# Two accumulation chains change places at the end of a 49-product in-projection

## The chip, the cores and the metric

The kernel runs on one core of a Trainium2 chip. The time is the device time of one launch in microseconds (us), as the median of several executions. A profile is one execution taken by the hardware profiler; its times run from the start of its span.

The engines are called TensorE (PE in the profile; its weight loads are PEld), VectorE (DVE), ScalarE (ACT), GpSimd (POOL) and SyncE (SP, which here only issues DMAs). TensorE writes PSUM, which is used as eight banks of 128 x 512 float32. The other engines work between PSUM and SBUF; in this kernel GpSimd only touches SBUF.

## The reference

Routed attention (4 batches, 8 heads, 768 positions, head size 64) is followed by a two-layer block on its 3072 x 512 output. The change touches only the second part, which computes

```
h  = x @ w_in                          # 3072 x 512 by 512 x 2048
sp = max(h, 0) + log1p(exp(-abs(h)))   # softplus
g  = h * erf(sp)
out = g @ w_out                        # 3072 x 2048 by 2048 x 512
```

## The kernel before

The attention takes about the first 430 us. Then the block runs in six chunks of 512 tokens (n = 0 to 5). Each chunk has an in-projection, which makes h transposed, a gate (Softplus, Erf, and a multiplication by h), and an out-projection.

**Fewer products by sums.** The projections are multiplied in the Strassen-Winograd manner: of 2 x 2 blocks, seven products instead of eight, at the price of sums and differences of blocks before and after. Chunks 3, 4 and 5 (`n >= TWICE`) use two such levels in the in-projection, 7 x 7 = 49 products; this is `hidden49` (line 1074). Chunks 1 and 2 run `hidden26`, with one level. Chunks 1 to 5 take the out-projection as 26 products (`project26`, line 1188).

**Slots.** `SLOTS` (line 118) lists the 49 products (i, o) in the order in which they run. i is the outer product and selects the weight form (`w_twice`); o is the inner one and selects the form of x. The list has three groups: i = 1 and 2 (slots 0 to 13), i = 6, 7 and 4 (slots 14 to 34), i = 5 and 3 (slots 35 to 48). In the last group the two chains run interleaved: (5,1), (3,1), (5,5), (3,5), (5,6), (3,6), (5,3), (3,3), (5,7), (3,7), (5,2), (3,2), (5,4), (3,4). A slot is four matmuls of 128 x 128 by 128 x 128 float32, recorded as eight.

**Banks and blocks.** The products of one i share banks: o = 1, 6, 7, 4 accumulate one after another into one bank, o = 5, 3 into a second, o = 2 has its own. The result must be read from the bank between two of them, so the next product of the chain waits for that reader. The results build up h in four pairs, called x, u, w and a fourth, y here (`WHERE`, line 115, gives the first three). Each has four blocks g11, g12, g21, g22 of 128 x 512.

**What follows a slot.** `copied` (line 1090): after o = 1, 5 and 6 ScalarE copies the bank to a place t (for x, w and u in this order); for i = 3 GpSimd then adds t to g12. `feed` (line 1104): after o = 2, 7 and 3, for i = 3 VectorE adds the bank to g12; for i = 5 VectorE adds the bank to t, and GpSimd then adds t to g22 and to g12. `feed_last` (line 1126): after o = 4 VectorE adds the bank to blocks of y: g12 for i = 3, g22 and g12 for i = 5. All of this is one line in the profile, L130, a helper that keeps each engine's instructions in program order. So an instruction that waits holds all that come later on its engine.

**Work between slots.** The table `also` (line 1145) places other work after given slots. `soft1`, `erf1`, `products1` gate the first half of the early blocks (half of h, called lot 0, is finished early), `soft2`, `erf2`, `products2` the second half; one Softplus or Erf works on 128 x 1024, and one product on 128 x 512 (four for each half). Their curves stand in one buffer, `a_s`; its pool has one place, so the next user of it (`soft_late`, line 1045, after slot 47) can't write before the fourth of `products2` has read it. `soft_late(n, 1)` is the Softplus of two late quarters of h; `gate_after` (line 1054) continues with two more, and then Erf and products during `project26`. `first_steps` are three sums of gated blocks (first entries of `LEFT_STEPS`, line 73); the third of them makes the left operand of the out-product p = 2 (`LEFT`, line 69: 17, 13, 18, ...). It writes the place that the copies (3,x) and (3,u) held before. The out-product p = 1 needs the second of `products2`, p = 8 and p = 9 need late products and further steps.

Softplus and Erf have different tables on ScalarE; the compiler puts a table load in front of an instruction whose function is not in the table that is loaded.

**Weight forms.** The second level needs differences of weight blocks. `forms_twice` (line 962) makes those for i = 5, 6 and 4 on GpSimd during chunk 2, in four places (the two `osb` buffers, halved), and stores them to `w_dram` on SP's queue; `hidden49` reads them back in a ring (`load_twice`). The form for i = 7 stays in SBUF: `last_form_twice` (line 976) writes it over b12, seven subtractions on GpSimd between the in- and the out-projection of chunk 2.

In the step numbers below "slot" counts from 0 to 48 in a chunk, and p from 0 to 25 in its out-projection.

Of the kernel before, what the change touches and what calls it, by code (L numbers as in the profile page):

```python
# [9 lines left out]
F32 = mybir.dt.float32  # L10
# [5 lines left out]
ACT = mybir.ActivationFunctionType  # L16
# [3 lines left out]
P = 128  # L20
# [16 lines left out]
FG = HF // 2  # L37
# [76 lines left out]
STEPS = (1, 5, 6, 3, 7, 2, 4)  # L114
WHERE = {"x": (0, 0), "u": (0, 1), "w": (1, 1)}
TWICE = 3
GROUPS = (((1, 2), (1, 5, 6, 3, 7, 2, 4)), ((6, 7, 4), (1, 2, 5, 6, 3, 7, 4)), ((5, 3), (1, 5, 6, 3, 7, 2, 4)))
SLOTS = [(i, o) for inner, outer in GROUPS for o in outer for i in inner]
STREAMED = [s for s in SLOTS if s[0] in (4, 5, 6)]

# [18 lines left out]
def kernel(  # L139
# [10 lines left out]
    nc = tc.nc  # L150

    in_order = [True]
    te, ve, ae, ge = (
        InOrder(tc, e, in_order) for e in (nc.tensor, nc.vector, nc.scalar, nc.gpsimd)
    )
# [6 lines left out]
    dram = pool("dram", 1, space=bass.MemoryType.DRAM)  # L162
# [102 lines left out]
    for base, pattern, sign, op, fill in (  # L265
# [5 lines left out]
            out=first, in_=first, compare_op=op, fill=fill, base=base, pattern=pattern,  # L271
# [19 lines left out]
    places = [x_of[n][:, i : i + 2].rearrange("p k t -> p (k t)") for n in range(2) for i in (0, 2)]  # L291
# [327 lines left out]
    def minus_of(out, a, b, engine=ve):  # L619
        engine.tensor_tensor(out=out, in0=a, in1=b, op=ALU.subtract)  # L620
# [74 lines left out]
    def onto(out, m, engine=ve):  # L695
        plus_of(out, m, out, engine)
# [118 lines left out]

    ring, extra = [], []
    x_extra, spare_more = {}, []
    w_dram = dram.tile([len(STREAMED), P, FG * P], F32, name="w_dram")
    b_dram = dram.tile([N_STREAM + len(KEPT), P, FG * HM], F32, name="b_dram")

    def w_block(b):
# [140 lines left out]
    def forms_twice():  # L962
        places = [outp.tile([P, 2, DM], F32, name="osb").rearrange("p h m -> p (h m)") for _ in range(2)]
        places = [t[:, i * FG * P : (i + 1) * FG * P] for t in places for i in range(2)]
        n = 0
        for o in STEPS:
            w = lefts(*w_in_parts(0, HF))[o]
            b11, b12, b21, b22 = (w[:, k, f * FG * P : (f + 1) * FG * P] for k in range(2) for f in range(2))
            new = [places[(n + i) % 4] for i in range(3)]
            n += 3  # L970
            for i, form, a, b in ((5, minus_of, b12, b11), (6, minus_of, b22, new[0]), (4, minus_of, new[1], b21)):
                t = new[{5: 0, 6: 1, 4: 2}[i]]
                form(t, a, b, ge)
                nc.sync.dma_start(out=w_dram[STREAMED.index((i, o))], in_=t)

    def last_form_twice():
        for o in STEPS:
            w = lefts(*w_in_parts(0, HF))[o]
            b12, b22 = (w[:, k, FG * P :] for k in range(2))
            minus_of(b12, b22, b12, ge)  # L980

    def x_twice(n):
        own = x_of[n].rearrange("p (k i) (t j c) -> p k i t j c", k=2, i=2, j=2, c=P)
# [90 lines left out]
    def hidden49(n):  # L1074
        if banks[0] is None:
            banks[:] = [psb.tile([P, 512], F32, name="bank") for _ in range(6)] + turned
        k = n_banks[0] + 1
        free = [banks[(k + i) % len(banks)] for i in range(len(banks))]
        x_extra[n] = xp.tile([P, DM // P, CT], F32, name="x_own")
        x_forms, x_form = x_twice(n)  # L1080
        for lot in range(2):
            for s in range(2):
                g_of[n, s, lot] = gp.tile([P, 2, 2, FG, P], F32, name="g")
        kept = [outp.tile([P, 2, DM], F32, name="osb").rearrange("p h m -> p (h m)") for _ in range(2)]
        kept = [t[:, i * FG * P : (i + 1) * FG * P] for t in kept for i in range(2)]
        temps = [columns(extra[i]) for i in range(3)] + kept
        fixed = {(5, "x"): kept[0], (5, "w"): kept[1], (5, "u"): kept[2], (3, "x"): temps[2], (3, "w"): kept[3], (3, "u"): temps[2]}
        chain, second, held = {}, {}, {}

        def copied(i, which, m):  # L1090
            t = held[i, which] = fixed[i, which] if (i, which) in fixed else temps.pop(0)
            ae.copy(out=t, in_=m)
            if i == 3:
                ge_onto(gs(WHERE[which])[1], t)

        def gs(c):

            h, s = c
            return [columns(block_of(n, h, s, lot, tt)) for tt in range(2) for lot in range(2)]

        def ge_onto(out, a):
            ge.tensor_tensor(out=out, in0=out, in1=a, op=ALU.add)

        def feed(i, which, m):
            g11, g12, g21, g22 = gs(WHERE[which])
            if i == 3:
                onto(g12, m)
                return
            t = held.pop((i, which))
            dst = {1: g12, 2: g11, 7: g22, 4: g21}.get(i, t)  # L1110
            plus_of(dst, m, t)
            if i == 2:
                ge_onto(g11, g12)
            elif i == 6:
                ge_onto(g12, t)
            elif i == 7:
                ge_onto(g22, g12)
            elif i == 4:
                minus_of(g21, g22, g21, ge)
            elif i == 5:  # L1120
                ge_onto(g22, t)
                ge_onto(g12, t)
            if (i, which) not in fixed:
                temps.append(t)

        def feed_last(i, m):
            g11, g12, g21, g22 = gs((1, 0))
            if i == 1:
                ae.copy(out=g12, in_=m)
            elif i == 2:  # L1130
                plus_of(g11, m, g12)
            elif i in (6, 3):
                onto(g12, m)
            elif i == 7:
                plus_of(g22, m, g12)
            elif i == 4:
                minus_of(g21, g22, m)
            else:
                onto(g22, m)
                onto(g12, m)  # L1140

        soft1, erf1, products1 = gate_early(n, 0)
        soft2, erf2, products2 = gate_early(n, 1)
        first_steps = [functools.partial(left_step, n, x) for x, step in enumerate(LEFT_STEPS) if step[0] < 0]
        also = {
            0: x_forms[0:2], 1: x_forms[2:3], 2: x_forms[3:4], 3: x_forms[4:6], 4: x_forms[6:7], 5: x_forms[7:8],
            10: [soft1[1]], 14: [soft1[0]], 15: [erf1[1]], 16: [erf1[0]],
            20: products1[0:1], 21: products1[1:2], 22: products1[2:3], 23: products1[3:4],
            33: [soft2[1]], 36: [soft2[0]], 37: first_steps[0:1], 38: first_steps[1:2], 40: [erf2[1], erf2[0]],
            43: products2[0:1], 44: products2[1:2], 45: products2[2:3] + first_steps[2:], 46: products2[3:4],  # L1150
            47: [functools.partial(soft_late, n, 1)],
        }
        for at, (i, o) in enumerate(SLOTS):
            w, x = w_twice(n, i, o), x_form(i, o)
            if o in (1, 2, 5):
                m = free.pop(0)
                if o != 2:
                    (chain if o == 1 else second)[i] = m
            else:
                m = (second if o == 3 else chain)[i]  # L1160
            for j in range(FG):
                te.matmul(
                    m[:, j * P : (j + 1) * P], lhsT=w[:, j * P : (j + 1) * P], rhs=x,
                    start=(o in (1, 2, 5) and j == 0), stop=(j == FG - 1), skip_group_check=True,
                )
            if (i, o) in STREAMED:
                k = STREAMED.index((i, o))
                if k + 6 < len(STREAMED):
                    load_twice(n, k + 6)
                else:  # L1170
                    for j in range(RING):
                        tile_of = (N_STREAM * (n - 1) + j + 2) % RING
                        if max(q for q in range(len(STREAMED)) if tile_twice(n, q) == tile_of) == k:
                            load_stream(N_STREAM * (n - 1) + j)
            if o in (1, 5, 6):
                copied(i, {1: "x", 5: "w", 6: "u"}[o], m)
            elif o == 4:
                feed_last(i, m)
            else:
                feed(i, {2: "x", 7: "w", 3: "u"}[o], m)  # L1180
            if o in (2, 3, 4):
                free.append(m)
            for f in also.get(at, ()):
                f()
        banks[:] = free
        n_banks[0] = len(banks) - 1
# [235 lines left out]
    for e in range(2):  # L1422
        ve.tensor_copy(
            out=ccT[e * D : (e + 1) * D, :, e * C : (e + 1) * C],
            in_=pct[e * D : (e + 1) * D].rearrange("d (r e c) -> d r e c", e=2, c=C)[:, :, e],
# [171 lines left out]
```

## Time and profile before

| | before |
|---|---|
| median of 3 executions | 993.03 us (992.92 to 994.28) |
| the profiled execution | 994.45 us |
| its span | 992.7 us |
| PE busy | 964.9 us (97%) |
| DVE, ACT, POOL busy | 780.3 us, 545.8 us, 532.3 us |
| ACT table loads | 42 by the compiler, 1283 ns each |
| chunk 4, slots 0 to 46 and before (793.4 to 836.0) | PE busy 42.29 of 42.60 us |
| chunk 4, slot 47 to p = 8 (836.0 to 861.5) | PE busy 20.75 of 25.50 us, clock 0.87 |
| chunk 4, p = 9 and on (861.5 to 891.3) | PE busy 29.79 of 29.80 us |

The timeline's rows give start, duration, engine, line, operation, and the program's names of output and inputs (`bank` and `turned` are PSUM banks; `g` is h; `g_more`, `osb` and `x_own` are places that are used in turn for several things). In brackets stands the idle time of the engine before the row and what ended it.

The chain of waits is followed back from the last instruction. Its rows give start, duration, and the engine or cause. The table of stretches gives, for each, its length, each engine's busy share, the granted clock of TensorE (1.00 is full), the share of the DMA engines and GB/s.

### The profile page before, as it was taken

Reading aid. Unit: us, or ns where it says so; the run is one execution under the profiler, and the core shown is the slowest. Engines: PE = TensorE matmul, PEld = TensorE weight load, DVE = VectorE, ACT = ScalarE, POOL = GpSimd, SP = SyncE. Lnnn points to the kernel's source line nnn. Section 1 sums busy time; section 2 is a strip of 40 time slices with the busy share of each in tenths; the row PEclk is TensorE's granted clock in tenths of the full one; section 3 lists DMA queues with packets and bytes.
Section 4 is the critical chain, followed back from the end, with each engine's and each line's share of the span. In section 5 each row is a group of like instructions: output and inputs, shape, how many; then the busy total and the mean of one; then the engine's idle time right before and its main releaser. Section 6 shows DMA issues by size and latency. Waiting matters only on the chain.

```text
span 992.7 us, 22118 instructions
## 1 busy us (share of the span) xinstructions
PE 964.9 (97%) x8786; PEld 731.5 (74%) x8786; DVE 780.3 (79%) x1372; ACT 545.8 (55%) x835; POOL 532.3 (54%) x368
## 2 busy tenths in 40 slices
PE   8999999999999999999999999989989998999898
PEld 3555555555555555788888888878987898789877
DVE  8888888888888886889698785778757965796577
ACT  3777777777776665585424523542635263526351
POOL 1688888787888888662499306530361037003700
PEclk9999999999999999999999999999999999999999
DMA  9444444444444210331024535214451445243423
GB/s 220 82 110 108 109 108 113 110 116 104 95 95 108 53 34 18 109 112 52 1 86 178 183 136 193 107 52 140 138 192 64 146 131 181 67 164 120 128 85 106
DMA packets 169287, 110.53 MB, mean 111 GB/s; under 512 B 131040, under 2 KB 140768, under 8 KB 169184
## 3 DMA queue, kind: packets, MB, share of 16 engines
q1 hardware_dynamic: 166688, 108.69, 38.1%
q8 instruction: 69, 1.13, 0.5%
q10 hardware_dynamic: 2496, 0.43, 0.2%
q14 instruction: 34, 0.28, 0.1%
HBM read 84.71 MB, written 24.38 MB: 110 GB/s over the span
## 4 chain that ended last, share of the span: by engine, by line
PE 89%; ACT 4%; DVE 3%; POOL 2%; issue 1%; DMA 1%; POOLq 0%; DVEq 0%; ACTq 0%; SPq 0%
PE bank L130 38%; PE turned L130 29%; PE sc L130 16%; PE wide L130 6%; POOL g L130 2%; ACT a_s L130 1%; ACT x_own L130 1%; DVE nmx L130 1%; ACT L130 1%; DVE osb L130 1%; DVE g L130 1%; ACT g_more L130 0%; ACT osb L130 0%; DMA g_more<-b_dram 0%; DVE g_more L130 0%
## 5 line engine op out<-in xcount | busy, mean ns | idle before, releaser
L130 POOL TENSOR_TENSOR more_out<-more_out,pr 128x768 f32<-128x768 f32 x128 | 217.1, 1696 | 18.5 <-ACT pr L130 10.0
L130 DVE TENSOR_REDUCE nmx<-wide 128x2 f32<-128x768 f32 x189 | 180.6, 955 | 47.8 <-PE wide L130 47.0
L130 ACT ACTIVATE pr<-sc 128x768 f32<-128x768 f32 x192 | 148.9, 811 | 93.9 <-PE wide L130 77.0
L130 PE MATMUL turned<-pr,in_v 128*32 128x193 f32 x3072 | 144.8, 330 | 0.0
L130 PEld LDWEIGHTS turned<-pr,in_v 128*32 128x32 f32 x3072 | 91.5, 109 | 50.7 <-issue 21.3
L130 POOL TENSOR_TENSOR g<-g 128x512 f32<-128x512 f32 x27 | 35.4, 1311 | 162.4 <-DVE g L130 161.0
L130 PE MATMUL sc<-qT,kT 64*128 64x384 f32 x528 | 98.3, 486 | 0.0
L130 DVE TENSOR_TENSOR g<-a_s,g 128x512 f32<-128x512 f32 x84 | 75.9, 926 | 21.6 <-ACT a_s L130 21.6
L130 ACT ACT_TABLE_LOAD x42 | 53.9, 1283 | 65.8 <-DVE g L130 65.2
L130 DVE TENSOR_TENSOR g<-g 128x512 f32<-128x512 f32 x114 | 78.9, 692 | 13.5 <-PE bank L130 12.1
L130 DVE TENSOR_TENSOR g<-bank,g 128x256 f32<-128x256 f32 (+1 forms) x133 | 58.6, 457 | 38.1 <-POOL g L130 13.0
L130 PE MATMUL bank<-g_more,g 128*128 128x256 f32 x336 | 79.8, 380 | 3.5 <-ACT g_more L130 3.5
L130 PE MATMUL bank<-x_own,w_in 128*128 128x256 f32 (+1 forms) x416 | 77.5, 327 | 0.0
L130 POOL TENSOR_TENSOR more_out<-pr,pr 128x768 f32<-128x768 f32 x32 | 60.3, 1886 | 28.3 <-ACT pr L130 28.3
L130 PEld LDWEIGHTS bank<-g_more,g 128*128 128x128 f32 x336 | 63.3, 190 | 13.9 <-ACT g_more L130 4.7
L130 PE MATMUL bank<-w_out,g 128*128 128x256 f32 x296 | 69.3, 380 | 0.0
L130 PEld LDWEIGHTS bank<-x_own,w_in 128*128 128x128 f32 x416 | 64.2, 191 | 6.0 <-issue 0.6
L130 PEld LDWEIGHTS <-qv 64*128 64x128 bf16 x384 | 27.0, 93 | 52.9 <-issue 36.8
L130 PEld LDWEIGHTS sc<-qT,kT 64*128 64x128 f32 x528 | 49.9, 187 | 21.4 <-ACT inv L130 2.4
L130 PE MATMUL wide<-kv,qv 64*128 64x384 bf16 x378 | 64.0, 328 | 1.4 <-DVE nmx L130 0.6
L130 ACT ACTIVATE a_s<-g 128x1024 f32<-128x1024 f32 (+1 forms) x38 | 42.7, 1146 | 37.6 <-POOL g L130 34.6
L130 PE MATMUL wide<-km,qm 64*128 64x384 bf16 (+1 forms) x378 | 62.6, 327 | 0.0
(235 smaller groups left out, 2051.5 us busy)
## 6 DMA issues: line engine op xcount, KB each, us to landing
g_more<-b_dram SPq DMA_DIRECT2D x48, 512.0 KB, 3.2
g_more<-w_dram SPq DMA_DIRECT2D x63, 256.0 KB, 2.8
x_own<-in_moe_w_in_dram SPq DMA_DIRECT2D x13, 512.0 KB, 4.5
in_v<-in_v_dram SPq DMA_DIRECT2D x32, 192.0 KB, 3.0
x_dram<-more_out SPq DMA_DIRECT2D x128, 48.0 KB, 1.9
x_own<-x_dram SPq DMA_DIRECT2D x6, 1024.0 KB, 5.5
in_k<-in_k_dram SPq DMA_DIRECT2D x59, 96.0 KB, 2.6
in_q<-in_q_dram SPq DMA_DIRECT2D x58, 96.0 KB, 2.6
```

Of the source, the lines that this page charges most:

```text
L130: ins = getattr(self.engine, name)(*args, **kw)
```

## The change

Five things are done:

1. The last group of slots runs i = 3 before i = 5: (3,1), (5,1), (3,5), (5,5) and so on to (3,4), (5,4).
2. The bank copies of (3,w) and (5,w), after slots 37 and 38, go from ScalarE to VectorE. The add of t to g12 after (5,2) goes from GpSimd to VectorE.
3. The Softplus table is loaded by an instruction of its own after slot 8 and after slot 40.
4. In `also`, the first two `first_steps` come after slots 35 and 36 (before: 37 and 38), the first Erf after slot 38 (before: 40), `products2` after slots 42, 44, 46 and 48 (before: 43 to 46), and the third first step after slot 48, behind the fourth product (before: slot 45).
5. `forms_twice` also makes and stores the form for i = 7 (28 subtractions and stores instead of 21), and `last_form_twice` loads it over b12 with seven DMAs of 256 KB instead of subtracting in place.

```diff
-GROUPS = (((1, 2), (1, 5, 6, 3, 7, 2, 4)), ((6, 7, 4), (1, 2, 5, 6, 3, 7, 4)), ((5, 3), (1, 5, 6, 3, 7, 2, 4)))
+GROUPS = (((1, 2), (1, 5, 6, 3, 7, 2, 4)), ((6, 7, 4), (1, 2, 5, 6, 3, 7, 4)), ((3, 5), (1, 5, 6, 3, 7, 2, 4)))
...
-    w_dram = dram.tile([len(STREAMED), P, FG * P], F32, name="w_dram")
+    w_dram = dram.tile([len(STREAMED) + len(STEPS), P, FG * P], F32, name="w_dram")
...
-            new = [places[(n + i) % 4] for i in range(3)]
-            n += 3
-            for i, form, a, b in ((5, minus_of, b12, b11), (6, minus_of, b22, new[0]), (4, minus_of, new[1], b21)):
-                t = new[{5: 0, 6: 1, 4: 2}[i]]
-                form(t, a, b, ge)
-                nc.sync.dma_start(out=w_dram[STREAMED.index((i, o))], in_=t)
+            new = [places[(n + i) % 4] for i in range(4)]
+            for t, i, a, b in (
+                (new[0], 5, b12, b11), (new[1], 6, b22, new[0]), (new[2], 4, new[1], b21), (new[3], 7, b22, b12),
+            ):
+                minus_of(t, a, b, ge)
+                k = STREAMED.index((i, o)) if i < 7 else len(STREAMED) + STEPS.index(o)
+                nc.sync.dma_start(out=w_dram[k], in_=t)
 
     def last_form_twice():
         for o in STEPS:
             w = lefts(*w_in_parts(0, HF))[o]
-            b12, b22 = (w[:, k, FG * P :] for k in range(2))
-            minus_of(b12, b22, b12, ge)
+            nc.sync.dma_start(out=w[:, 0, FG * P :], in_=w_dram[len(STREAMED) + STEPS.index(o)])
...
             t = held[i, which] = fixed[i, which] if (i, which) in fixed else temps.pop(0)
-            ae.copy(out=t, in_=m)
+            if which == "w" and i in (3, 5):
+                ve.tensor_copy(out=t, in_=m)
+            else:
+                ae.copy(out=t, in_=m)
...
                 ge_onto(g22, t)
-                ge_onto(g12, t)
+                if which == "x":
+                    onto(g12, t)
+                else:
+                    ge_onto(g12, t)
...
-            10: [soft1[1]], 14: [soft1[0]], 15: [erf1[1]], 16: [erf1[0]],
+            8: [functools.partial(ae.preload_act_table, ACT.Softplus)], 10: [soft1[1]], 14: [soft1[0]], 15: [erf1[1]], 16: [erf1[0]],
             20: products1[0:1], 21: products1[1:2], 22: products1[2:3], 23: products1[3:4],
-            33: [soft2[1]], 36: [soft2[0]], 37: first_steps[0:1], 38: first_steps[1:2], 40: [erf2[1], erf2[0]],
-            43: products2[0:1], 44: products2[1:2], 45: products2[2:3] + first_steps[2:], 46: products2[3:4],
-            47: [functools.partial(soft_late, n, 1)],
+            33: [soft2[1]], 35: first_steps[0:1], 36: [soft2[0]] + first_steps[1:2], 38: [erf2[1]],
+            40: [erf2[0], functools.partial(ae.preload_act_table, ACT.Softplus)],
+            42: products2[0:1], 44: products2[1:2], 46: products2[2:3], 47: [functools.partial(soft_late, n, 1)],
+            48: products2[3:4] + first_steps[2:],
```

## The prediction

> **What bounds the kernel now.** I read the page's chain of waits first. TensorE sets almost the whole span, so only the places where TensorE is idle or slow can give time back:
>
> ```profile
> PE 89%; ACT 4%; DVE 3%; POOL 2%; issue 1%; DMA 1%; POOLq 0%; DVEq 0%; ACTq 0%; SPq 0%
> ```
>
> The changed slots run in chunks 3, 4 and 5. One chunk lasts 97.8 us: the out-product p=9 starts at 763.75, 861.51 and 959.28 us in the timeline of PE. I work in chunk 4. TensorE runs slots 35 to 46 without a gap and ends slot 46 at 835.7. Up to p=9 it has two slots of 0.89 and nine products of 1.73 us to do, 17.3 us; it needs 25.8. So 8.5 us per chunk are lost there, and that is all this change can win back. The chain of waits, in order of time, names who holds them:
>
> ```profile
> 836.18 0.69 DVE osb L130
> 836.94 2.87 POOL g L130 x2
> 839.87 0.57 issue
> 840.44 0.68 DVE g L130
> 841.12 0.61 DVE osb L130
> 841.80 3.33 POOL g L130 x2
> 845.15 1.30 DVE g L130 x2
> 846.54 1.28 ACT L130
> 847.84 0.66 ACT a_s L130
> ```
>
> VectorE hands a block to GpSimd, waits for it, hands over the next, then ScalarE loads a table and starts Softplus. The timeline of VectorE shows the queue behind it:
>
> ```profile
> 835.57 0.69 DVE L130 TENSOR_TENSOR g<-bank,g 128x512 f32<-128x512 f32 x1 [3.55 <-POOL g L130]
> ...
> 839.83 0.69 DVE L130 TENSOR_TENSOR g<-turned,g 128x512 f32<-128x512 f32 x1 [2.37 <-POOL g L130]
> ...
> 842.23 1.76 DVE L130 TENSOR_TENSOR g_more<-g,g_more 128x512 f32<-128x512 f32 x1
> 845.15 0.69 DVE L130 TENSOR_TENSOR g<-bank,g 128x512 f32<-128x512 f32 x1 [1.16 <-POOL g L130]
> 845.76 0.68 DVE L130 TENSOR_TENSOR g<-a_s,g 128x512 f32<-128x512 f32 x1
> ```
>
> The first, second and fourth rows are slots 42, 44 and 46, chain i=3: they add into the same g12 block into which GpSimd has just been told to add i=5 (slots 41, 43, 45). The last row is the fourth early product; it reads the only a_s buffer, and the late Softplus writes that buffer next:
>
> ```profile
> 846.54 1.28 ACT L130 ACT_TABLE_LOAD   x1 [11.75 <-DVE g L130]
> 847.84 2.01 ACT L130 ACTIVATE a_s<-g 128x1024 f32<-128x1024 f32 x2
> ```
>
> The load starts 0.10 us after that product ends (845.76+0.68=846.44). Chunks 3 and 5 repeat it (748.67 to 748.77, 944.21 to 944.31), so the end T of the fourth product, not the slots' copies, releases ScalarE. From Softplus's start to p=9 it is 861.51-847.84=13.67 us of four Softplus, a load, four Erf and VectorE's work behind them. So p=9 = T+0.10+1.30+13.67.
>
> **Part 1, i=3 before i=5.** No count changes. Now the i=3 add into g12 stands ahead of the i=5 adds to the same block, so VectorE's three waits above (3.55, 2.37, 1.16) go. What is late next: slot 41, now (3,3), adds into the u block's g12, and GpSimd must first add the u copy of slot 39 there. So I follow ScalarE from 826.56, where Softplus still starts on the same GpSimd add: copies of slots 35 and 36 at 827.5 and 828.0, Softplus 828.46 to 829.53, the Erf load moved forward 829.54 to 830.82, Erf to 831.89, u copy of slot 39 from 831.79 to 832.38. GpSimd adds it, 1.27 (row 830.58): 833.7. VectorE starts slot 41 at 833.73. Before, the same kind of wait ended at 835.54.
>
> From there VectorE has fourteen instructions up to the fourth product: nine with a bank as operand (slots 41 to 47 one each, slot 48 two), the added g12 add of (5,x), and four products. Their pitch is 0.60 (841.03, 841.63, 842.23), so 8.45 us and T=842.2 if nothing holds them.
>
> **The price of GpSimd beside them.** Two rows speak. An add from SBUF alone took 1.76 while GpSimd's two took 3.32 (rows 842.23 and 841.80) instead of 0.68 and 2.50: they take turns. Adds with a bank operand keep 0.69 in the same company (820.46). Five GpSimd adds now fall into this stretch (both of u, both of w, one of x), and five VectorE instructions are from SBUF alone. No row shows this order. Below: no collision, T=842.2. Above: each of the five waits out a whole add, 5x1.27=6.35, T=848.55. I take turns, one after the other, as those rows do: product 1 at 834.93 goes first; product 2 at 836.73 meets GpSimd's end, no loss; the (5,x) add waits to 838.6; product 3 waits 839.13 to 840.4; product 4, at 842.65, waits for GpSimd's last add until 843.45. T=844.05, nearer to the lower end.
>
> **Part 2, tables.** The load at slot 40 lands 833.8 to 835.1 on an idle ScalarE, so Softplus follows T directly: 1.30 less. The other load, moved to slot 8, saves nothing: in the trace it already ran at 799.62, 5 us ahead of its Softplus, while GpSimd was awaited. Without the cover of that idle ScalarE each costs 1.28. [...]
>
> **Part 3, the copies of (3,w) and (5,w) on VectorE.** Two bank copies, bounded by a half-size bank copy, 0.42, and a full add, 0.69; I take 0.69, the size. They fall at 827.8 and 828.6, where VectorE was idle 3.46 us (row 831.33). Cost nothing; the cover gone, 1.2. They take 0.9 us off ScalarE ahead of the u copies, which is in the times above.
>
> **Part 4, first step 3 moved behind product 4.** The third out-product, p=2, needs it: 844.05+0.65=844.7. TensorE ends p=1 near 841.5, so it idles 3.2 us there. From 844.7 seven products of 1.725 reach p=9 at 856.8, before ScalarE's path (844.05+0.05+13.67=857.8). But a gap can slow TensorE. The trace has such a case after gaps of 1.22 and 2.50 us (slot 48, p=0 and p=1 in PE's timeline, then one microsecond of the table of stretches, where the number after the five engines is the granted clock):
>
> ```profile
> 840.58 2.08 PE L130 MATMUL turned<-g_more,w_in 128*128 128x128 f32 x8 [2.50 <-DVE g L130]
> 842.45 3.62 PE L130 MATMUL bank<-more_out,g_more 128*128 128x256 f32 x8
> 845.86 1.98 PE L130 MATMUL bank<-w_out,g 128*128 128x256 f32 x8
> ```
> ```profile
> 844.00:845.00 1.00, 1.00 (x3) 0.74 (x3) 0.00 (x0) 0.00 (x0) 1.00 (x1) 0.50 0.00 0
> ```
>
> The clock (the 0.50) is halved for some 5 us, and 3.62 instead of 1.89 is one product's price. Chunk 2's gap of 2.10 us (663.32) brought no loss. Paid again, p=9 moves to 856.8+1.73=858.5, 0.8 later; I take 0 and keep 0.8. [...]
>
> **Part 5, resident forms.** Seven more GpSimd subtractions with seven 256 KB stores in chunk 2; seven reloads replace the seven in-place subtractions. The 21 old ones run 604.1 to 633.1, so 28 end near 644, still before the osb places are wanted (first write after 650). While they run, VectorE's four products at 634.89 to 638.02 lengthen from 0.69 to 1.42, as at 620.22 to 625.28: ScalarE's next load moves 639.12 to 641.8, 2.67 later. Against that the in-place ones no longer sit beside the products at 646.89 to 651.99 (1.48, 1.42, 1.10, 1.42), 2.67 back. The sum is about 0; one half alone bounds it at -2.7 and +2.7. The stores and reloads share SP's queue. The reloads wait for TensorE's last read of w_in (647.3) and take about 0.45 each to issue, done by 650.5; the next entry there was issued at 654.35. First use is in chunk 3's slots 14 and on, over 50 us later. One landing (2.8 us) is what it would cost without this.
>
> **Sum.** Per chunk (846.44-844.05)+1.38=3.77, three chunks 11.3, chunk 2 nothing. The profiled execution took 994.45 us, its span 992.7; that is 1.4 above the median of 993.03. The difference applies to either: 994.45-11.3=983.1, and for the median 981.7.
>
> **Rivals.**
> *Only the table goes.* GpSimd's turns and the late u copy leave T at 846.44: 3x1.38=4.1, 988.9 us. For it: five turns instead of four; against: VectorE starts 1.8 us earlier.
> *Nothing moves.* The preload is followed by another load and T stays: 993.0. For it: no row shows this table loaded without a function behind it; against: copies between Softplus and loads needed no table in the trace (799.62 to 804.67).
> *Slower, by GpSimd's turns.* In slots 42 to 48 every SBUF-only VectorE instruction loses its turn: T=848.55, p=9 at 862.3, 0.73 late, 995.2 us. It decides against the change once T passes 847.8. For it: the 1.76 row; against: products at 836.77 and 841.63 won theirs.
>
> **How the numbers follow.** Forecast 0.75, 981.7 us, with T between 843 and 845.5 (978.6 to 986.1) and chunk 2 at its bounds 976 to 989; only the table 0.11; nothing 0.05; slower 0.09. Range 976 to 989: it holds the forecast and about half of the first rival. Under 0.2% (2.0 us) a measurement here cannot tell a change from none: faster 0.86, same 0.05, slower 0.09.
>
> **What would show it.** Right: the distance between two p=9 starts falls from 97.8 to 94.0; the Softplus on a_s at the end has no load in front; VectorE waits once, until about 9 us after slot 35's start, for the u add; TensorE idles near 3 us before p=2, released by g_more. Wrong: T's product behind long GpSimd turns, a half clock at p=2, or a stall in chunk 2 beyond the 2.1 us of p=8.

## The result and the profile after

The changed kernel took 988.81 us in the median of 5 executions (988.33 to 989.38), the kernel before beside it 993.04. The ratio is 0.9956, with a 95% interval of 0.9941 to 0.997: faster by 4.4 us, between 3.0 and 5.9. A second sample of it, beside other runs of the kernel before, gave 0.9956 again (0.9942 to 0.997). Forecast were 11.3 us, so the sign was right and the size was not.

The profiled execution took 988.33 us (span 986.6), against 994.45 for the profiled one before. The traces therefore differ by 6.1 us and the medians by 4.2. The kernel before came out between 992.63 and 995.05 in its runs beside the experiments, and its profiled execution lies high in that band. What makes that spread isn't settled; the granted clock, 0.989 to 0.993 in them, doesn't order them. (One more execution of it, left out of all ratios, took 1108.48 us at a granted clock of 0.851.) The working below explains the 6.1 us of the traces.

First the page's chain of waits, by engine:

```profile
PE 89%; DVE 6%; ACT 2%; issue 2%; POOL 1%; DMA 0%; DVEq 0%; SPq 0%; ACTq 0%; POOLq 0%
```

GpSimd fell from 2% to 1% and ScalarE from 4% to 2%, as intended; VectorE rose from 3% to 6%. The chain in order of time in chunk 4 shows how (start, duration, engine):

```profile
829.78 0.48 ACT g_more L130
830.26 0.07 issue
830.33 1.28 POOL g L130
831.61 0.02 issue
831.63 0.04 DVE g L130
...
837.66 5.74 DVE g L130 x6
843.40 0.61 DVE g_more L130
844.01 0.04 issue
844.05 5.21 PE bank L130 x16
```

There is now one hand-over instead of three: the u copy on ScalarE, GpSimd's add, and then VectorE alone for 12 us until the third first step lets TensorE start p=2. VectorE's timeline says what it does with those 12 us:

```profile
831.63 0.69 DVE L130 TENSOR_TENSOR g<-bank,g 128x512 f32<-128x512 f32 x1 [4.56 <-POOL g L130]
...
834.64 1.79 DVE L130 TENSOR_TENSOR g<-a_s,g 128x512 f32<-128x512 f32 x1
...
837.66 1.67 DVE L130 TENSOR_TENSOR g<-osb,g 128x512 f32<-128x512 f32 x1
839.25 1.75 DVE L130 TENSOR_TENSOR g<-a_s,g 128x512 f32<-128x512 f32 x1
...
842.72 0.68 DVE L130 TENSOR_TENSOR g<-a_s,g 128x512 f32<-128x512 f32 x1
843.32 0.68 DVE L130 TENSOR_TENSOR g_more<-g,g_more 128x512 f32<-128x512 f32 x1
```

It waits once (the bracket of the first row). But product 2, the (5,x) add and product 3 take 1.79, 1.67 and 1.75 instead of 0.68 (I read a long duration without a bracket as a wait inside the instruction; without GpSimd's adds the same three take 0.68 or 0.69, below). All three read SBUF only, and GpSimd's five i=5 adds fill the same stretch:

```profile
833.00 7.45 POOL L130 TENSOR_TENSOR g<-g,osb 128x512 f32<-128x512 f32 x5 [1.40 <-DVE osb L130]
```

In a window that holds one add alone (834.7 to 835.7), the same view shows the second of the five:

```profile
834.61 1.27 POOL L130 TENSOR_TENSOR g<-g,osb 128x512 f32<-128x512 f32 x1
```

It starts 0.03 us before product 2 (834.64) and ends at 835.88; product 2 ends 0.55 later, at 836.43. In the same way the (5,x) add ends 0.56 after GpSimd's fourth add (838.77), and product 3 ends 0.54 after the fifth (840.46). GpSimd pays too: its first, third and fifth add, each behind a VectorE instruction of this kind, take 1.65, 1.72 and 1.71 instead of 1.27.

ScalarE's timeline shows the table load on idle time and Softplus directly behind product 4 (842.72+0.68=843.40):

```profile
831.71 1.28 ACT L130 ACT_TABLE_LOAD   x1
843.51 2.00 ACT L130 ACTIVATE a_s<-g 128x1024 f32<-128x1024 f32 x2 [10.52 <-DVE g L130]
```

And TensorE's timeline, with one microsecond of the table of stretches (the number after the five engines is the granted clock):

```profile
837.80 1.89 PE L130 MATMUL bank<-w_out,g 128*128 128x256 f32 x8
844.05 3.48 PE L130 MATMUL bank<-w_out,g_more 128*128 128x256 f32 x8 [4.37 <-DVE g_more L130]
...
856.01 1.89 PE L130 MATMUL bank<-w_out,g_more 128*128 128x256 f32 x8
857.74 1.89 PE L130 MATMUL bank<-g_more,g 128*128 128x256 f32 x8
```
```profile
845.00:846.00 1.00, 1.00 (x4) 0.75 (x3) 0.52 (x1) 1.00 (x2) 0.00 (x0) 0.50 0.00 0
```

Nothing holds TensorE in slots 47 and 48 any more, but there is a single gap of 4.37 us ahead of p=2, then a halved clock, and p=9 (the last row) starts without a wait. Two p=9 starts lie 95.7 us apart (761.99, 857.74, 953.39), against 97.8 before and 94.0 forecast.

**One yardstick for all kernels.** Chunk 4 starts at another time in every kernel. So I count from S, the start of the first first step on VectorE, an instruction that all kernels have (825.53 before, 823.41 after). T is again the end of the fourth product. All rows are from chunk 4 of the profiled execution.

| kernel | T-S | gap before p=2 | p=9 minus S | T-S + 13.77 (+ 1.30 if the load is late) |
|---|---|---|---|---|
| before | 20.91 | 0 | 35.98 | 35.98 |
| changed | 19.99 | 4.37 | 34.33 | 33.76 |
| before, table early | 20.89 | 0 | 34.69 | 34.66 |
| changed, table late | 20.01 | 4.38 | 35.06 | 35.08 |
| changed, TensorE kept busy | 19.99 | 0.92 | 33.77 | 33.76 |
| changed, five adds left out | 16.86 | 1.21 | 30.62 | 30.63 |
| changed, u copy on VectorE | 18.18 | 3.52 | 33.76 | 31.95 |
| changed, product 4 earlier | 18.81 | 3.18 | 33.35 | 32.58 |
| both of these | 16.99 | 2.32 | 30.77 | 30.76 |
| both, (5,x) add on GpSimd | 15.78 | 2.19 | 30.62 | 29.55 |
| changed, old order of chains | 22.52 | 0.08 | 36.31 | 36.29 |
| changed, w copies on ScalarE | 20.95 | 4.37 | 35.49 | 34.72 |

13.77 is 0.10 from T to Softplus and 13.67 on to p=9, from the trace of before. Where the last two columns agree, ScalarE's path sets p=9. Where they don't, TensorE came later (or, in one kernel, something new). "Gap" counts only an idle TensorE directly ahead of p=2.

### The profile page after: what moved, and what is told of

It is laid out like the page before. It is cut to its first block, busy times and chain, and to the rows that moved or that the text cites. A ratio compares the mean times of both kernels' runs of the same rounds, so it can differ in the third digit from the quotient of the medians.

```text
span 986.6 us, 22145 instructions
## 1 busy us (share of the span) xinstructions
PE 962.0 (98%) x8786; PEld 730.8 (74%) x8786; DVE 792.1 (80%) x1381; ACT 541.9 (55%) x829; POOL 528.8 (54%) x365
## 4 chain that ended last, share of the span: by engine, by line
PE 89%; DVE 6%; ACT 2%; issue 2%; POOL 1%; DMA 0%; DVEq 0%; SPq 0%; ACTq 0%; POOLq 0%
PE bank L130 37%; PE turned L130 29%; PE sc L130 16%; PE wide L130 6%; DVE g L130 4%; ACT a_s L130 1%; DVE nmx L130 1%; DVE osb L130 1%; POOL g L130 1%; ACT L130 1%; ACT g_more L130 0%; DVE g_more L130 0%; ACT osb L130 0%; DMA in_q<-in_q_dram 0%; DVE sims L130 0%
## 5 line engine op out<-in xcount | busy, mean ns | idle before, releaser
L130 DVE TENSOR_TENSOR g<-a_s,g 128x512 f32<-128x512 f32 x84 | 82.2, 1000 | 20.5 <-ACT a_s L130 20.5
L130 PE MATMUL bank<-x_own,w_in 128*128 128x128 f32 (+1 forms) x464 | 84.1, 323 | 1.1 <-ACT g_more L130 1.1
L130 PEld LDWEIGHTS bank<-x_own,w_in 128*128 128x128 f32 x464 | 70.0, 191 | 7.8 <-ACT g_more L130 1.7
```

Of the source, the lines that this page charges most:

```text
L130: ins = getattr(self.engine, name)(*args, **kw)
```

## The experiments

The theory after the result, called theory 1: p=9 is the later of ScalarE's path (T+13.77) and TensorE's path from p=2, which includes the halved clock; and T is set by VectorE's queue, lengthened by three turns with GpSimd. The rival: only the table load was saved, and the rest of the change came to nothing. Gains are (1 - ratio) x 993 us, against the kernel before on the same chip.

### The table alone, and everything but the table

In the kernel before, the load added after slot 40:

```diff
-40: [erf2[1], erf2[0]],
+40: [erf2[1], erf2[0], functools.partial(ae.preload_act_table, ACT.Softplus)],
```

> The kernel before, with one edit: the Softplus table is loaded behind the second Erf of slot 40. Theory 1 (two paths): the end T of the fourth product stays, ScalarE's path to p=9 is 1.38 us shorter in each of three chunks, and TensorE's own path (p=1 at 845.86 and eight products) allows 859.7 against 860.1, so 4.1 us are won: 988.9. Theory 2 (only the table counts in the whole change): the same 988.9, all that the change brought. If the load was covered after all: 993.0.

Measured: 991.12 us, ratio 0.9968 (0.9956 to 0.998), a gain of 3.2 (2.0 to 4.4) that holds the expected 4.1. In the trace p=9 minus S falls by 1.29, the load to a hundredth. The profiled execution lost some 0.6 us to a reduced clock at p=8 and p=9 of chunk 2 (2.45 and 2.85 us instead of 1.97 each), a chunk whose code the edit doesn't touch.

The reverse, the changed kernel without the load at slot 40:

```diff
-40: [erf2[0], functools.partial(ae.preload_act_table, ACT.Softplus)],
+40: [erf2[0]],
```

> The changed kernel without the load behind slot 40; the compiler's load is back in front of the late Softplus. Theory 1: p=9 is the later of TensorE's path (857.7 in chunk 4 of the changed kernel) and ScalarE's path (857.2); only the second moves, by 1.3 to 858.5, so 0.74 a chunk is lost, 2.2 in all: 991.0. Theory 2: all 4.1 us are lost, 993.0.

Measured: 991.56 us, ratio 0.9978 (0.997 to 0.9987). 2.2 us of the gain remain without the table, so the rival falls. The compiler's load stands in front of Softplus again (844.34), and with it ScalarE's path is the later one. That is why the load's 1.30 is worth only 0.73 per chunk here (35.06 against 34.33): with it gone from ScalarE's path, TensorE's decides.

### GpSimd's turns

The changed kernel without GpSimd's five i=5 adds. It leaves those five sums of 128 x 512 per chunk out of h.

```diff
-ge_onto(g22, t)
 if which == "x":
     onto(g12, t)
-else:
-    ge_onto(g12, t)
```

> The changed kernel without GpSimd's five adds of chain i=5 (u and w into g22 and g12, x into g22), so part of h is left out; all else stays. Theory 1 (three VectorE instructions wait out a GpSimd add: 1.79, 1.67, 1.75 instead of 0.68): they take 0.68, T is 3.1 us earlier, the gap before p=2 about 1.3, the clock full; ScalarE's path decides and 3.4 a chunk are won, 10 in all: 979. Rival (the three are long for another reason, as their place in memory or the DMAs then under way): T stays within 0.5, above 987.

Measured: 977.97 us, ratio 0.984 (0.9826 to 0.9854), a gain of 15.9 against the 14 expected. The same three instructions, and product 4, in VectorE's timeline of this kernel:

```profile
831.35 0.68 DVE L130 TENSOR_TENSOR g<-a_s,g 128x512 f32<-128x512 f32 x1
...
833.26 0.69 DVE L130 TENSOR_TENSOR g<-osb,g 128x512 f32<-128x512 f32 x1
833.87 0.68 DVE L130 TENSOR_TENSOR g<-a_s,g 128x512 f32<-128x512 f32 x1
...
836.27 0.68 DVE L130 TENSOR_TENSOR g<-a_s,g 128x512 f32<-128x512 f32 x1
```

From slot 41's add to T it is 8.60 us (828.35 to 836.95), and 11.77 with the adds. The difference, 3.17, is the sum of the three excesses (1.11, 0.99, 1.07). So the long instructions are the company of GpSimd, and that is all that lengthens the queue.

### The halved clock

The changed kernel with eight more matmuls into p=2's own bank directly ahead of p=2, which overwrites them:

```diff
+if n >= TWICE and p == 2:
+    for f in range(8):
+        te.matmul(m, lhsT=w_in[:, 0, 0:P], rhs=w_out[:, 0, 0:HM], start=True, stop=True)
```

> The changed kernel with eight additional matmuls into p=2's own bank ahead of p=2 in chunks 3 to 5, 3.45 us of TensorE work in the 4.4 us gap; their result is overwritten. Theory 1: the clock stays full, p=2 takes 1.73 instead of 3.4, TensorE's path to p=9 ends 856.1, ScalarE's 857.2 decides, 0.56 a chunk is won, 1.7 in all: 987.1. Theory 2: 988.8, no change. If the additional matmuls end after p=2's operand is ready, they cost what they are late.

Measured: 987.87 us, ratio 0.9939 (0.9926 to 0.9952), a gain of 6.1 where 5.9 was expected. The timeline of TensorE:

```profile
838.13 3.62 PE L130 MATMUL bank<-w_out,w_in 128*128 128x256 f32 x16
842.67 1.99 PE L130 MATMUL bank<-w_out,g_more 128*128 128x256 f32 x8 [0.92 <-DVE g_more L130]
...
855.79 1.96 PE L130 MATMUL bank<-g_more,g 128*128 128x256 f32 x8 [0.77 <-ACT g_more L130]
```

With useless work in the gap (the first row, the eight matmuls, recorded as sixteen) p=2 keeps its full speed (1.99 us), and p=9 waits for ScalarE again, at T+13.77 to 0.01 us. The gain over the changed kernel is small, because ScalarE's path is only 0.57 shorter than TensorE's.

### An earlier start and a shorter queue

Two mends that theory 1 offers. The copy of (3,u) on VectorE, so that GpSimd's add of u, and slot 41, don't wait for ScalarE's Erf:

```diff
-if which == "w" and i in (3, 5):
+if which == "w" and i in (3, 5) or (i, which) == (3, "u"):
```

> The changed kernel with the bank copy of (3,u), slot 39, on VectorE too. Theory 1 (VectorE's queue sets T, and it starts when GpSimd has added the u copy): the copy no longer stands behind the Erf table load and an Erf, it ends near 828.0 instead of 830.2 in chunk 4, GpSimd's add near 829.8, VectorE goes on at 829.8 instead of 831.6. T is 1.8 earlier, the gap before p=2 2.6 instead of 4.4 us; with a full clock 2.3 a chunk are won, 7 in all: 982; with the clock still halved 1.7 a chunk: 983.6. Rival (GpSimd's five adds after slot 42 set T): they start with slot 42 in either case and need 7.45 us, so T moves by less than 1 and the time stays above 986.

Measured: 982.83 us, ratio 0.9887 (0.9871 to 0.9902): 11.2 us where 9.4 to 11 were expected. The profiled execution, 985.91 us, had a long halved clock; the other three took 982.25 to 982.93. Slot 41's wait falls from 4.56 to 1.77 and T-S by 1.81. The gap before p=2 missed its 2.6: it is 3.52, because TensorE's own p=1 came 0.95 earlier after S as well.

The fourth product and the third first step moved ahead of slot 48's two bank adds:

```diff
-47: [functools.partial(soft_late, n, 1)],
-48: products2[3:4] + first_steps[2:],
+47: products2[3:4] + first_steps[2:] + [functools.partial(soft_late, n, 1)],
```

> The changed kernel with the fourth product and the third first step ahead of the two adds of slot 48 instead of behind them. Theory 1: T and p=2 are 1.2 us earlier, with the clock still halved at p=2 p=9 is 1.2 earlier: 3.6 in all, 985.2. Rival (GpSimd's adds, done 840.45 in chunk 4, or the y block hold the Softplus): less than 0.5 a chunk, above 987.3.

Measured: 984.94 us, ratio 0.9913 (0.99 to 0.9926): 8.6 us, the expected 7.8 within the interval. T-S falls by 1.18.

Both together:

> The changed kernel with the two mends of the earlier runs together: the copy of (3,u) goes to VectorE as well, and the fourth early product with the third first step runs after slot 47, ahead of slot 48's two bank adds. Theory 1 (p=9 is the later of ScalarE's path, T+13.77, and TensorE's path from p=2): T and p=2 come 1.20 us earlier than with the copy alone, so p=2 starts at 839.45 after a gap of 2.3 us. If a gap of 2.3 us leaves the clock full, TensorE's path is 1.73 shorter too, ScalarE's path (about 852.6) decides, and p=9 comes 2.7 to 3.0 us per chunk earlier: 974 to 975 us. If the clock is still halved, only the 1.20 is won: 979.2. Rival (the two mends remove the same idle time): no better than the copy alone, 982 to 983.

Measured: 978.8 us, ratio 0.9849 (0.9836 to 0.9863): 15.0 us, faster than both kernels of this study. TensorE's timeline:

```profile
836.82 1.99 PE L130 MATMUL bank<-w_out,g_more 128*128 128x256 f32 x8 [2.32 <-DVE g_more L130]
...
849.95 1.96 PE L130 MATMUL bank<-g_more,g 128*128 128x256 f32 x8 [0.77 <-ACT g_more L130]
```

In chunks 3 and 4 the gap of 2.32 leaves the clock full and ScalarE's path decides, as the first branch said; p=9 minus S is 2.99 less than with the u copy alone. In chunk 5 a gap of 2.30 halves the clock (p=2 takes 2.61 us), and p=9 comes without a wait, 31.49 after S instead of 30.77. The time missed the first branch by 3 us. The expectation took its step from the median of the u-copy kernel, 982.83, while its numbers came from that kernel's profiled execution, 985.91, where the clock was halved for over 6 us in chunk 4. Between the two profiled executions p=9 comes 2.99 us earlier in chunk 3, 2.64 more in chunk 4 (a loss of 0.36 behind p=9 is told of below) and 2.12 more in chunk 5: 7.75 in all, the difference of 985.91 and 978.16.

### The other parts undone, one at a time

The old order of the chains, i=5 before i=3, in the changed kernel:

```diff
-((3, 5), (1, 5, 6, 3, 7, 2, 4))
+((5, 3), (1, 5, 6, 3, 7, 2, 4))
```

> The changed kernel with part 1 undone: chain i=5 before i=3 again, all else kept. Theory 1 (T is set by the length of VectorE's queue, whichever wait stands in it): of the three waits for GpSimd in the kernel before, that of x (1.16) stays away because its g12 add is now on VectorE, those of u and w come back; against that the turns beside GpSimd shrink. From T before, 846.44: less 1.16, less 1.76 (the first step behind the fourth product), plus 0.6 to 1.7 (the added add), plus 1.2 (slot 48's bank adds now ahead) gives 845.3 to 846.4, 0 to 0.9 later than the changed kernel: 988.5 to 991.5 us. Rival (the exchange of the chains carries the change, by the prediction's part 1): the three waits return whole, T some 3 us or more later, 998 us or above.

Measured: 995.44 us, ratio 1.0014 (1.0005 to 1.0023): slower than the kernel before, so the exchange is worth 5.8 us here. Both expectations missed: 1.0014 of 993 us are 994.4, some 3 us above theory 1's and 3.6 below the rival's. VectorE's timeline of this kernel:

```profile
832.58 0.69 DVE L130 TENSOR_TENSOR osb<-bank,osb 128x512 f32<-128x512 f32 x1 [3.22 <-ACT osb L130]
836.87 0.69 DVE L130 TENSOR_TENSOR g<-bank,g 128x512 f32<-128x512 f32 x1 [3.59 <-POOL g L130]
...
841.35 0.69 DVE L130 TENSOR_TENSOR g<-turned,g 128x512 f32<-128x512 f32 x1 [2.59 <-POOL g L130]
...
843.28 0.69 DVE L130 TENSOR_TENSOR g<-osb,g 128x512 f32<-128x512 f32 x1
```

Two of the three waits are back (3.59 and 2.59), and the turns are nearly gone (the last row is the (5,x) add, at 0.69). I had let the waits come back at their old size and place. But the first one now starts 1.07 later after S (6.87 instead of 5.80 in the kernel before), because the Erf that part 4 moved to slot 38, with its table load, stands ahead of the u copies on ScalarE: the first row's bracket names ScalarE, where before it was TensorE. By this trace the moved Erf needs the exchange; the old order with the Erf in its old place wasn't run.

The w copies back on ScalarE:

```diff
-if which == "w" and i in (3, 5):
-    ve.tensor_copy(out=t, in_=m)
-else:
-    ae.copy(out=t, in_=m)
+ae.copy(out=t, in_=m)
```

> The changed kernel with the copies of (3,w) and (5,w) back on ScalarE (the add of (5,x) stays on VectorE). Theory 1: they are two copies of some 0.5 us ahead of the u copy on ScalarE, so GpSimd's add of u, slot 41 on VectorE, T and p=2 all come about 0.9 us later: 2.7 us in three chunks, 991.5 us. Rival (ScalarE has idle time enough, since it then waits over 10 us for T): nothing, 988.8 us.

Measured: 993.74 us, ratio 0.9996 (0.9987 to 1.0005): the two copies are worth 4.0 us, against 2.7 expected. T-S is 0.96 longer, as expected (0.9). The rest fits the clock, which one profile of each can't show: in chunk 3 of the profiled execution it stayed halved through a second product (3.78 and 3.20 us for p=2 and p=3, against 3.65 and 1.89 in the changed kernel, but 3.78 and 2.53 in the changed kernel's second sample).

The weight forms of before (21 stores, the seven subtractions in place):

> The changed kernel with the weight forms of the kernel before (21 forms and stores, seven subtractions in place). Theory 1: the two halves of this part cancel, within 0.3 us: 988.8 to 989.1. Rival: the in-place subtractions beside the last products of chunk 2 were the dearer half: up to 2.7 us slower, 991.5; or the seven more forms were: 986.1.

Measured: 988.92 us, ratio 0.9949 (0.9935 to 0.9963), the same as the changed kernel within the intervals. Part 5 is worth nothing that could be measured.

The changed kernel once more, for the scatter:

> The changed kernel itself, on the same chip as the three that follow, as their measure: 988.8 by both theories (ratio to the kernel before 0.9956).

Measured: 989.45 us, ratio 0.9956, told at the top.

### A last try at a faster version

Both mends, and the (5,x) add back on GpSimd (`ge_onto(g12, t)` for all three blocks):

> The kernel with both mends (978.06 us against a kernel before of 993.04), with the g12 add of (5,x) back on GpSimd. Theory 1 (each SBUF-only VectorE instruction in the queue pays about one GpSimd add, whatever it is): in that kernel's chunk 4 the (5,x) add starts at 831.61 and holds VectorE 1.60; with it gone product 3 takes its turn at 831.61 to 833.29, a bank add follows, product 4 is asked for at 833.89 and waits for the fifth GpSimd add until 834.4. T is 835.1 instead of 836.17. The third first step then waits for the sixth add, so p=2 stays at 836.8; ScalarE's path gives p=9 at 848.9 and TensorE's the same, instead of 849.95: 1.0 per chunk, 975.0 us. Rival (a sixth GpSimd add costs the queue as much as the VectorE add did): T stays near 836.2, 977.5 to 978.5.

Measured: 978.85 us, ratio 0.9848 (0.9835 to 0.9861): no better than both mends alone. Yet T came 1.21 earlier, as theory 1 said. ScalarE's timeline shows where that went:

```profile
836.01 2.00 ACT L130 ACTIVATE a_s<-g 128x1024 f32<-128x1024 f32 x2 [6.79 <-DVE g L130]
838.89 2.00 ACT L130 ACTIVATE x_own<-g 128x1024 f32<-128x1024 f32 x2 [0.88 <-DVE g L130]
```

The third and fourth late Softplus now wait 0.88 for VectorE: they read the y blocks, whose two slot 48 adds stand behind the third first step, and that one met the sixth GpSimd add (1.76 at 835.82). Neither side of the expectation had this wait; the reader meets the next limit here. An order with the two adds ahead of the first step wasn't tried.

## Why the prediction was wrong in size

**What bounds the kernel, and the chain to p=9: right.** The formula T+0.10+13.67 (+1.30 with a late load) gives p=9 to 0.03 us in the seven kernels in which ScalarE's path decides (the table above).

**Part 1, the exchange: right.** VectorE starts slot 41 at 831.63. Forecast was 833.73, and chunk 4 runs 2.11 earlier here, so 831.62. The three waits are gone, and one for the u add stands in their place.

**The queue of fourteen instructions: right.** Forecast 8.45 us without GpSimd; 8.60 with the five adds left out.

**The price of GpSimd beside them: this step failed.** It read "product 2 meets GpSimd's end, no loss" and gave T=844.05. In those coordinates T was 843.40+2.11=845.51, 1.46 later and at the outer end of my own inner range. It let product 3 wait 1.27 and product 4 0.8, and product 2 and the (5,x) add next to nothing. Measured were 1.11 for product 2, 0.99 for the add and 1.07 for product 3, each about one GpSimd add, and nothing for product 4. Product 2 is where the schedule broke: I let it arrive just as a GpSimd add ended, and the tie went the other way, which cost 1.11. It did arrive there (834.64, the first add's end is 834.65), but GpSimd's second add had started at 834.61 and went first. Turns worked out to 0.1 us are one possible schedule. (By its own pitch of 0.60, product 3 should have asked at 839.20 and product 4 at 842.8, where I wrote 839.13 and 842.65; T stays 844.05.) Three whole waits of 1.27, between the bounds of none and five, would have given 846.0, which is nearer.

**Part 4, p=2 behind product 4: the second step that failed, made worse by the first.** With T 1.46 later the gap is 4.37 us instead of 3.2, the clock halves, and p=2 takes 3.48 us. I took 0 for that and kept 0.8. It put p=9 0.57 us behind ScalarE's path. The 3.2 us gap that I had forecast would not have been safe either: with product 4 earlier the gap was 3.17 or 3.18; in chunks 3 and 4 the clock halved (in chunk 4 p=2 and p=3 took 2.74 and 2.88 us, 0.77 behind ScalarE's path), in chunk 5 it stayed full. The 0 was my choice; no run shows that a 3.2 us gap is free in chunk 4. The row with the halved clock of the kernel before (3.62 us for one product) told more; the halving there lasted 6.83 us, not the 5 that I read.

**Part 2, tables: right.** 1.29 per chunk, with the table alone. The page still counts 42 loads, so none follows the added one; the load at slot 8 saves nothing (in the changed kernel it runs at 797.51, and its Softplus waits for GpSimd until 802.55, both 2.11 to 2.12 earlier than before, like the whole chunk).

**Part 3, the copies: right, and worth more than I said.** Free on VectorE; undone, they cost 4.0 us.

**Part 5, the forms: right.** p=9 of chunk 2 moves from 666.28 to 666.01.

**The sum.** At p=9 of chunk 4 the forecast comes to 861.51-857.77=3.74 us (the sum says 3.77: its 1.38 is 1.35 by the forecast's own terms; no run shows 1.38, the table alone brought 1.29). Of these 1.46 went to the turns, 0.57 to the clock, and 0.05 because I wrote 0.05 for the step from T to Softplus that is 0.10. The trace shows the rest, 1.66 (861.51-857.74-2.11). To it come 0.36 that I hadn't seen: after an awaited p=9 the products p=9 to p=11 run slower, and after is spared that. That makes 2.0 per chunk, and three of them are about the 6.1 us between the two traces.

**The range.** That 988.81 lies in the 976 to 989 is luck. T alone was given 978.6 to 986.1, and the rest was room for chunk 2, whose p=9 moved by 0.27 only. The clock's 0.57 a chunk and the 1.9 us by which the traces differ from the medians filled it.

**The rivals.** "Only the table goes" has the right time, 988.9, for a wrong reason. T did move, by 0.92, and without the table 2.2 us remained. That GpSimd's turns eat the gain was written down as its cause, and that much was so. "Nothing moves" falls with the table alone. "Slower" needed T past 847.8 and five whole waits; T came to 845.51 with three.

## What to carry to other kernels

When a change packs VectorE's work beside GpSimd's, count every VectorE instruction that has only SBUF operands and let each wait out a whole GpSimd add, unless the profile shows that it goes first (three of the five here took 0.99 to 1.11 us longer, beside adds of 1.27); instructions with a bank as operand ran free here (0.68). Before a producer of TensorE's next operand is moved later, work out the one gap that results: several short waits that grow into one long one can also pay in clock (in every case from 3.52 us on here, in some between 2.1 and 3.2), and a copy on a crowded engine ahead of the chain (here ScalarE's u copy) is worth as much as the waits themselves. And take the difference of two kernels from two profiled executions or from two medians, never from one of each.

## What the runs showed of the hardware

**SBUF company.** Three instructions of 128 x 512 from SBUF alone took 1.67 to 1.79 us on VectorE beside GpSimd's adds and 0.68 or 0.69 without them; adds with a bank as operand kept 0.68 in both. The three excesses (1.11, 0.99 and 1.07 us) come near one GpSimd add of 1.27 each, and of GpSimd's five adds three took 1.65 to 1.72. What makes the two engines wait for each other, the runs don't show.

**The clock's reaction isn't a fixed price of a gap.** In chunks 3 and 4, gaps of 3.17 to 4.38 us ahead of p=2 halved it in every profile, gaps of 0.92, 1.21, 2.19 and 2.32 in none. Chunk 5 turns this round: there 3.17 left it full (product 4 earlier), and 2.30 and 2.19 halved it (the two kernels with both mends). In chunk 2 a gap of 2.1 us ahead of p=8 halved it in the kernel with the table alone and not in the kernel before.

The idle time of TensorE, counted in stretches of 3.41 us, sorts these cases. In all profiles the halved stretches up to p=9 of chunk 5 last 3.41 or 6.83 us, and within an execution their starts lie whole multiples of 3.41 us apart (748.12, 843.69 and 939.26 in the changed kernel). In the table of stretches, cut at these starts, the first number after the length is TensorE's busy time. First the changed kernel in chunk 4, then the kernel with both mends in chunk 4 and in chunk 5:

```profile
840.28:843.69 3.41, 0.00 (x0) 0.00 (x0) 3.41 (x6) 0.18 (x1) 0.17 (x1) 1.00 0.00 0
843.69:847.10 3.41, 3.05 (x7) 2.51 (x8) 1.69 (x3) 3.41 (x4) 0.00 (x0) 0.50 0.00 0
```
```profile
835.01:838.42 3.41, 1.60 (x7) 1.44 (x8) 3.41 (x6) 2.14 (x3) 0.00 (x0) 1.00 0.00 0
838.42:841.84 3.42, 3.42 (x17) 3.02 (x16) 0.83 (x2) 3.39 (x5) 0.00 (x0) 1.00 0.13 22
```
```profile
927.17:930.58 3.41, 1.23 (x6) 1.11 (x7) 3.41 (x7) 1.77 (x2) 0.00 (x0) 1.00 0.00 0
930.58:933.99 3.41, 3.41 (x10) 2.70 (x9) 1.20 (x2) 3.39 (x5) 0.00 (x0) 0.50 0.00 0
```

Counted so in all 14 profiles, a stretch at full clock with 2.07 us or more of idle TensorE is followed by a halved one (32 cases, 2.07 to 3.41), and one with 1.91 or less never is. A halved stretch with 0.61 or more idle is followed by a second one, one with 0.53 or less never. So in these profiles it mattered where a gap fell among the stretches, and several short gaps in one stretch counted together: 1.22 and 2.50 in the kernel before put 2.26 into one (835.79 to 839.21), and the next was halved. From these counts I estimate for these kernels that a lone gap under 1.9 us is free, one over 4.1 (twice 2.07) pays, and one between pays or not by where it falls. Why the clock does this, the runs don't show.

From p=2 to p=9 it cost 1.61 us in chunk 4 of the changed kernel (13.69 instead of 7 x 1.725) and up to 3.2 in the one with the w copies on ScalarE. With the u copy on VectorE it was still full when p=2 began in chunk 3 and fell then, while in chunk 4 it was halved from the start (table of stretches, two answers):

```profile
746.00:747.00 1.00, 0.48 (x2) 0.46 (x3) 0.90 (x2) 1.00 (x2) 0.00 (x0) 1.00 0.00 0
747.00:748.00 1.00, 1.00 (x4) 0.85 (x4) 0.95 (x2) 1.00 (x3) 0.00 (x0) 0.62 0.00 0
```
```profile
840.00:841.00 1.00, 0.35 (x1) 0.35 (x2) 0.90 (x2) 0.89 (x1) 0.00 (x0) 0.50 0.00 0
```

So the same code with the same gap (3.53 and 3.52 us) paid at another moment and another price (1.8 and 2.9 us up to p=9). The four executions of this kernel took 985.91, 982.93, 982.74 and 982.25 us at a mean granted clock of 0.991, 0.996, 0.995 and 0.998; those with the five adds left out, where no such gap is, 977.67 to 978.43 at 0.999 to 1.000. A gap of this length also goes with a scatter of some us.

**A wait costs behind it, too.** Where p=9 waited, p=9, p=10 and p=11 started 1.85, 1.88 and 1.81 us apart at full clock (849.95, 851.80, 853.68, 855.49 with both mends) instead of 1.725, together 0.36 us. Two of TensorE's weight loads there stand behind "issue" (0.26 and 0.29 us in the kernel before, at 863.34 and 865.22). Why isn't settled.
